# GpSimd takes clamps and remainders of the weights' conversion in the first group, and ELU units are finished in PSUM

## The chip, the cores and the metric

The kernel runs on one core of a Trainium2 chip, as one program. Its engines are TensorE (PE in the profile, with its weight loads as PEld), VectorE (DVE), ScalarE (ACT), GpSimd (POOL), and SyncE (SP), whose queue issues most DMAs. The metric is the device time of one execution in microseconds, the median of three runs.

## The reference

Three stages on 6016 tokens of width 256:

```python
qn = q / (np.linalg.norm(q, axis=1, keepdims=True) + 1e-06)      # over the tokens
kn = k / (np.linalg.norm(k, axis=1, keepdims=True) + 1e-06)
s = kn.transpose(0, 2, 1) @ qn / tau                             # 256 x 256
a = np.exp(s - s.max(-1, keepdims=True)); a /= a.sum(-1, keepdims=True) + 1e-09
x = v @ a                                                        # 6016 x 256
h = x @ w_in                                                     # 256 -> 2048
g = np.where(h > 0, h, np.exp(np.minimum(h, 0)) - 1)             # ELU
x = g @ w_out                                                    # 2048 -> 256
h = x @ w2_in
out = (h / (1 + np.exp(-h))) @ w2_out                            # SiLU
```

The weights arrive as float64 and are read as pairs of 32-bit words.

## The kernel before

First the scores of q and k are summed over all tokens on TensorE, then the softmax is taken and folded into the first layer's input weights, so that the first layer works on v directly. After that the tokens go through layer 1 in six groups of up to 1024 and through layer 2 in six groups again, 12 groups in all. A group has eight steps (`NP`), each for two columns of 128 of the 2048 hidden units. In a step, `first_a` and `first_b` make four units (two halves of the tokens by two columns) of h in the PSUM banks h0 to h3, `unit` turns each into g, and `second` multiplies the g of the step before by the output weights and adds into the four PSUM banks y0 to y3, which hold the group's result over all its steps. Every matrix is held as a high part and a remainder, and a product is three matmuls (high by high, high by low, low by high).

The first group (`plain(n)`, n = 0) differs. Its products are not by a Strassen-like scheme as all others are, so a step has 24 matmuls for h instead of 21, and during it the weights of layer 1 are still being converted. `in_f32` turns a chunk of float64 weights into float32: two copies on ScalarE, a clamp (`ts` with min and max, line 440), a shift (441), the sign (442) and an addition of the low bits (443) on VectorE. `convert` then calls `split`: the high part is a copy on ScalarE, the remainder is a `tt` subtraction on VectorE (line 290). There are 16 chunks, eight of w_in ("w1i") and eight of w_out ("w1o"); the five in `EARLY` are begun ahead of the first step. Chunks of w_in are multiplied by the softmax on TensorE (`m_group`, into h banks), and the result is copied and split again (`m_parts`).

A unit of layer 1 (`unit`, lines 918 to 925) is a chain of five instructions: relu of -h on ScalarE (e from h), exp on ScalarE (e from e), `stt` on VectorE (e from e and h, max(e - 1, h)), a copy on ScalarE to g's high part, and a `tt` on VectorE for g's remainder. h lies in a PSUM bank, e in one of four SBUF buffers.

The first step is special too: its third and fourth unit have no h bank left and are made in y2 and y3 (`first_step`, `y_bank(2), y_bank(3)`). The first `second` then writes y2, y3, y0, y1 in this order. y0 and y1 hold at that time a product of the softmax with the weights (`m_first`), which ScalarE copies out (the rows `h<-y,small`).

The order of the instructions on each engine isn't that of the code. `do` records each one with a cost and with what it reads and writes, and `in_order` then makes a list schedule from a table of costs per engine (`COST`); the engines run what it gives in that fixed order, each waiting at the head of its queue. A PSUM bank is one key: it may be written by the next product when all that read or wrote it for the last one is done.

Of the kernel before, what the change touches and what calls it, by code (L numbers as in the profile page):

```python
# [16 lines left out]
ALU = mybir.AluOpType  # L17
# [4 lines left out]
EARLY = ("w1i", 0), ("w1i", 1), ("w1o", 0), ("w1i", 2), ("w1i", 3)  # L22
# [4 lines left out]
TOP = float(np.array(0x0FEFFFFF, np.uint32).view(np.float32))  # L27
# [16 lines left out]
    "PE": (0.0127, 1 / 2400, 0.22, 0.0),  # L44
    "ACT": (0.14, 1 / 1400, 0.18, 0.12),
    "DVE": (0.067, 1 / 960, 0.15, 0.19),
    "SP": (0.37, 0, 2.3, 0.0),
    "-": (0.0, 0, 0.0, 0.0),
}
# [2 lines left out]
V = namedtuple("V", "ap keys")  # L52
# [102 lines left out]
def channel_attention_elu_silu(  # L155
# [28 lines left out]
    nc = tc.nc  # L184
# [38 lines left out]
    def f32(ap):  # L223
        return ap.bitcast(F32)
# [6 lines left out]
    def do(engine, n, emit, reads, writes, times=1, far=0.0):  # L231
        fixed, each, late, own = DENSE if dense and engine == "ACT" else COST[engine]
        late += far
        ops.append(
            Op(
                engine,
                times * (fixed + each * n),
                late,
                own,
                emit,  # L240
                [k for v in reads if isinstance(v, V) for k in v.keys],
                [k for v in writes for k in v.keys],
                hot,
            )
        )

    def width(ap):
        return int(np.prod(ap.shape[1:]))

    def at(x):  # L250
        return real(x.ap) if isinstance(x, V) else x
# [17 lines left out]
    def tt(out, a, b, op):  # L269
        do("DVE", width(out.ap), lambda: nc.vector.tensor_tensor(at(out), at(a), at(b), op), [a, b], [out])  # L270

    def ts(out, a, s1, s2, *op):
        do("DVE", width(out.ap) / 2, lambda: nc.vector.tensor_scalar(at(out), at(a), at(s1), at(s2), *op), [a, s1, s2], [out])  # L273

    def stt(out, a, s, b, op0, op1):
        emit = lambda: nc.vector.scalar_tensor_tensor(at(out), at(a), at(s), at(b), op0, op1)  # L276
        do("DVE", width(out.ap), emit, [a, s, b], [out])
# [7 lines left out]
        queue, engine = (nc.scalar, "ACT") if by == "ACT" else (nc.sync, "SP")  # L285
        do(engine, 0, lambda: queue.dma_start(at(out), at(src)), [src], [out], n if engine == "SP" else 2 + 3 * short, far)  # L286

    def split(hi, lo, src):
        copy(hi, src)
        tt(lo, src, V(f32(hi.ap), hi.keys), ALU.subtract)  # L290

    def product(out, lhs, rhs, start=True, stop=True, **kw):

# [90 lines left out]
    def wo_at(part, i):  # L384

        also = tuple(("eT", part, d) for d in range(CT)) if i == NP - 1 else ()
        if i in (5, 6):
            also = tuple(("w1i", part, x) for x in range(2))
        return V(wo[part][:, 2 * i : 2 * i + 2], (("wo", part, i), *also))
# [39 lines left out]
    def in_f32(name, i, *order, far=0.0, after=(), wait=()):  # L429


        raw = load(name, i, *order, far=far, after=after)
        low, high = src_of.pop((name, i))
        t = cvs.take()
        a, b = low.ap.shape[1:3]
        w = V(t.ap.rearrange("p (a b) -> p a b", a=a), t.keys)
        wi = V(w.ap.bitcast(I32), t.keys)
        copy(w, V(f32(high.ap), high.keys + wait), scale=2.0**-112)
        copy(low, V(low.ap.bitcast(U32), low.keys + wait), scale=2.0**-29)
        ts(w, w, TOP, -TOP, ALU.min, ALU.max)  # L440
        ts(wi, wi, 3, None, ALU.logical_shift_left)
        stt(wi, V(high.ap, high.keys), SIGN, wi, ALU.bitwise_and, ALU.bitwise_or)
        tt(V(flat(wi.ap), wi.keys), V(flat(wi.ap), wi.keys), V(flat(low.ap), low.keys), ALU.add)
        return w, raw

    def convert(name, i, *order, wait=(), far=LATE[0]):
        w, _ = in_f32(name, i, *order, far=far if order else 0.0, wait=wait)
        if name == "w1i":
            s = slice(i % 2 * HC, (i % 2 + 1) * HC)
            hi, lo = (w1i_at(i // 2, a, slice(None), i % 2) for a in range(2))  # L450
            split(V(hi.ap[:, :, s], hi.keys), V(lo.ap[:, :, s], lo.keys), w)
        else:
            split(wo_at(0, i), wo_at(1, i), w)

    def put_by(name, i, s):

# [33 lines left out]
    with tc.manual_schedule():  # L490
# [87 lines left out]
        for i, (j0, nj) in enumerate(rows):  # L578
            for a, src in enumerate((qv, kv)):
                v = rows_at(a, j0, nj)  # L580
                by = "ACT" if a and i < len(ENDS[0]) else "SP"
                order = ("order",) if by == "SP" else ("order_k",)
# [248 lines left out]
        def plain(n):  # L831

            return n == 0
# [72 lines left out]
        def unit(s, u, h):  # L906
            n, j = steps[s]
            m = cols(n)
            e = cols_of(es.take(), m)
            i = g_free.pop(0)  # L910
            if i < 6:
                g = [V(gs[:, i, a, :m], (("g", i, a),)) for a in range(2)]
            else:
                g = [wa_at(a, i, slice(S1, S4 + 1)) for a in range(2)]
                g = [V(x.ap.flat(), x.keys) for x in g]
            g_at[s, u] = i, g
            if order[n][0] == 1:
                act(e, h, AF.Relu, scale=-1.0)
                act(e, e, AF.Exp, scale=-1.0)
                stt(e, e, -1.0, h, ALU.add, ALU.max)  # L920
                copy(g[0], e)
            else:
                act(g[0], h, AF.Silu)
                act(e, h, AF.Silu)
            tt(g[1], e, V(f32(g[0].ap), g[0].keys), ALU.subtract)
# [328 lines left out]
```

## Time and profile before

| | |
|---|---|
| runs | 1037.5, 1037.96, 1038.38 us; median 1037.96 us |
| span of the profiled execution, first to last instruction | 1035.8 us |
| granted clock of TensorE | 1.00 of full in all 40 slices |
| TensorE busy | 1030.4 us, 99% |
| VectorE, ScalarE, GpSimd busy | 825.1, 749.4, 0.7 us |

The profiled execution's own time isn't listed beside its span; the median of the runs lies 2.2 us above the span, and a difference in the span is carried over to it. Matmuls are pipelined: their listed durations overlap, and it is the distance between starts that tells what one costs. The first group runs from about 53 to 158 us after the span's start.

### The profile page before, as it was taken

The numbers are of one execution on the slowest core, as the hardware profiler recorded it, in microseconds if no ns is written. First come the engines' busy times: TensorE is split into PE (matmuls) and PEld (weight loads), VectorE is DVE, ScalarE is ACT, GpSimd is POOL, SyncE is SP. The second block draws the span as 40 slices with busy tenths as digits, with TensorE's granted clock in tenths as the row PEclk, the third lists the DMA queues.
The fourth block names the chain that finished last, engine by engine and source line by source line (L and its number), as shares of the span: only waits on it lengthen the run. The fifth ranks groups of instructions, "written<-read, shape, count | busy, mean of one in ns | idle before, by whom it ended". The sixth has DMA issues, their size and how long they took to land.

```text
span 1035.8 us, 13366 instructions
## 1 busy us (share of the span) xinstructions
PE 1030.4 (99%) x4734; PEld 872.4 (84%) x4734; DVE 825.1 (80%) x1401; ACT 749.4 (72%) x1410; POOL 0.7 (0%) x6
## 2 busy tenths in 40 slices
PE   9999999999999999999999999999999999999998
PEld 8888888888888888888998888998888888888887
DVE  6999999999989989989998866667566657657553
ACT  6799988989788888888897765565565556555543
POOL 0000000000000000000000000000000000000000
PEclk9999999999999999999999999999999999999999
DMA  9663332033032113013434003012003003001102
GB/s 379 220 173 113 112 71 102 1 72 112 18 75 103 51 46 102 31 42 122 135 97 156 11 1 82 1 41 37 1 4 78 1 1 82 1 1 22 20 1 41
DMA packets 112389, 71.38 MB, mean 69 GB/s; under 512 B 87874, under 2 KB 90562, under 8 KB 111682
## 3 DMA queue, kind: packets, MB, share of 16 engines
q1 hardware_dynamic: 109584, 68.96, 22.6%
q10 hardware_dynamic: 2738, 1.57, 0.5%
q8 instruction: 37, 0.61, 0.3%
q14 instruction: 30, 0.25, 0.1%
HBM read 49.81 MB, written 20.71 MB: 68 GB/s over the span
## 4 chain that ended last, share of the span: by engine, by line
PE 99%; ACT 0%; ACTq 0%; DVE 0%; issue 0%
PE y L297 50%; PE h L297 44%; PE y L324 4%; PE h L311 1%; PE h L324 0%; PE y L311 0%; PE h L329 0%; ACTq L286 0%; ACT big L256 0%; PE y L329 0%; ACT h L256 0%; ACT a L256 0%; DVE a L276 0%; DVE ones L491 0%; ACT e L256 0%
## 5 line engine op out<-in xcount | busy, mean ns | idle before, releaser
L297 PE MATMUL y<-gs,wo 128*128 128x512 f32 (+1 forms) x2196 | 520.5, 385 | 0.0
L297 PEld LDWEIGHTS y<-gs,wo 128*128 128x128 f32 x2196 | 411.8, 188 | 78.1 <-ACT e L256 0.8
L297 PE MATMUL h<-xs,wa 128*128 128x512 f32 (+1 forms) x1980 | 472.6, 385 | 0.0
L297 PEld LDWEIGHTS h<-xs,wa 128*128 128x128 f32 x1980 | 370.9, 188 | 68.5
L270 DVE TENSOR_TENSOR gs<-e,gs 128x512 fp32r<-128x512 f32 (+1 forms) x382 | 253.2, 676 | 90.9 <-ACT e L256 88.6
L270 DVE TENSOR_TENSOR h<-h,h 128x512 f32<-128x512 f32 (+1 forms) x352 | 228.0, 678 | 80.2 <-PE h L297 62.3
L256 ACT ACTIVATE e<-h 128x512 f32<-128x512 f32 (+2 forms) x383 | 225.5, 600 | 46.1 <-DVE h L270 43.5
L256 ACT ACTIVATE h<-h 128x512 f32<-128x512 f32 (+1 forms) x176 | 103.6, 589 | 136.8 <-PE h L297 136.7
L256 ACT ACTIVATE gs<-h 128x512 fp32r<-128x512 f32 (+1 forms) x192 | 116.5, 607 | 70.0 <-DVE h L270 37.7
L276 DVE SCALAR_TENSOR_TENSOR e<-e,h 128x512 f32<-128x512 f32 (+1 forms) x190 | 123.0, 671 | 18.2 <-ACT e L256 17.7
L256 ACT ACTIVATE e<-e 128x512 f32<-128x512 f32 (+1 forms) x192 | 114.0, 623 | 1.3
L256 ACT ACTIVATE gs<-e 128x512 fp32r<-128x512 f32 (+1 forms) x190 | 110.7, 624 | 1.6 <-DVE e L276 1.6
L270 DVE TENSOR_TENSOR xs<-big,xs 128x512 fp32r<-128x512 f32 (+1 forms) x77 | 50.2, 672 | 0.0
L256 ACT ACTIVATE xs<-big 128x512 fp32r<-128x512 f32 (+1 forms) x77 | 45.4, 623 | 1.0 <-DVE big L270 0.7
L270 DVE TENSOR_TENSOR sums<-sums 128x2048 f32<-128x2048 f32 (+3 forms) x17 | 29.4, 1727 | 7.2 <-ACT sums L256 6.2
L273 DVE TENSOR_SCALAR cv<-cv 128x512 f32<-128x512 f32 (+1 forms) x64 | 26.4, 422 | 0.6 <-ACT cv L256 0.3
L297 PEld LDWEIGHTS y<-wo,gs 128*128 128x128 f32 x192 | 24.7, 191 | 1.0
L297 PE MATMUL y<-wo,gs 128*128 128x256 f32 x192 | 25.1, 283 | 0.0
L256 ACT ACTIVATE cv<-st 128x512 f32<-128x512 f32 x32 | 21.4, 674 | 1.5 <-DMA st<-in_moe_w_in_dram 1.5
L324 PE MATMUL y<-ring 128*128 128x256 f32 x92 | 22.3, 395 | 0.0
L276 DVE SCALAR_TENSOR_TENSOR cv<-st,cv 128x512 int32<-128x512 int32 x32 | 21.9, 687 | 0.4
L270 DVE CUSTOM_DVE_ANT_0 cv<-st,cv 128x1024 uint16<-128x1024 uint16 x32 | 21.9, 686 | 0.0
(100 smaller groups left out, 369.6 us busy)
## 6 DMA issues: line engine op xcount, KB each, us to landing
st<-in_moe_w_in_dram SPq DMA_DIRECT2D x16, 512.0 KB, 3.9
st<-in_moe_w_out_dram SPq DMA_DIRECT2D x16, 512.0 KB, 3.8
yd<-e SPq DMA_DIRECT2D x20, 256.0 KB, 2.4
big<-yd SPq DMA_DIRECT2D x5, 1024.0 KB, 4.7
big<-in_v_dram SPq DMA_DIRECT2D x32, 128.0 KB, 3.5
wod<-st SPq DMA_DIRECT2D x8, 512.0 KB, 2.9
wo<-wod SPq DMA_DIRECT2D x8, 512.0 KB, 4.0
out_dram<-big SPq DMA_DIRECT2D x32, 128.0 KB, 2.9
```

The lines of the kernel that those rows point to most:

```text
L256: nc.scalar.activation(at(out), at(src), func, **{k: at(x) for k, x in kw.items()}, **more)
L270: do("DVE", width(out.ap), lambda: nc.vector.tensor_tensor(at(out), at(a), at(b), op), [a, b], [out])
L273: do("DVE", width(out.ap) / 2, lambda: nc.vector.tensor_scalar(at(out), at(a), at(s1), at(s2), *op), [a, s1, s2], [out])
L276: emit = lambda: nc.vector.scalar_tensor_tensor(at(out), at(a), at(s), at(b), op0, op1)
L297: nc.tensor.matmul(at(out), at(lhs[a]), at(rhs[b]), start=start and a + b == 0, stop=stop and a == 1, **kw)
L311: nc.tensor.matmul(at(out), at(both[n][0][a]), at(both[n][1][b]), start=(n, a, b) == (0, 0, 0), stop=(n, a) == (1, 1),)
L324: emit = lambda: nc.tensor.matmul(at(out), at(lhs), at(rhs), start=start, stop=stop, **kw)
```

## The change

Two things. In the first group's conversions, GpSimd now makes the remainders of all eight chunks of w_out and of the six chunks of w_in that aren't the first two (14 subtractions), and the clamps of the eleven chunks that aren't in `EARLY`. `COST` has a row for GpSimd, and the schedule is made anew. And in the first group's units, the `stt` writes its result over h in the PSUM bank instead of into e; the copy and the remainder read it from there.

```diff
--- before.py
+++ after.py
@@ -44,6 +44,7 @@
     "PE": (0.0127, 1 / 2400, 0.22, 0.0),
     "ACT": (0.14, 1 / 1400, 0.18, 0.12),
     "DVE": (0.067, 1 / 960, 0.15, 0.19),
+    "POOL": (0.2, 2.2 / 1000, 0.2, 0.12),
     "SP": (0.37, 0, 2.3, 0.0),
     "-": (0.0, 0, 0.0, 0.0),
 }
@@ -269,7 +270,10 @@
     def tt(out, a, b, op):
         do("DVE", width(out.ap), lambda: nc.vector.tensor_tensor(at(out), at(a), at(b), op), [a, b], [out])
 
-    def ts(out, a, s1, s2, *op):
+    def ts(out, a, s1, s2, *op, pool=False):
+        if pool:
+            do("POOL", width(out.ap) * 0.7, lambda: nc.gpsimd.tensor_scalar(at(out), at(a), at(s1), at(s2), *op), [a], [out])
+            return
         do("DVE", width(out.ap) / 2, lambda: nc.vector.tensor_scalar(at(out), at(a), at(s1), at(s2), *op), [a, s1, s2], [out])
 
     def stt(out, a, s, b, op0, op1):
@@ -285,9 +289,13 @@
         queue, engine = (nc.scalar, "ACT") if by == "ACT" else (nc.sync, "SP")
         do(engine, 0, lambda: queue.dma_start(at(out), at(src)), [src], [out], n if engine == "SP" else 2 + 3 * short, far)
 
-    def split(hi, lo, src):
+    def split(hi, lo, src, pool=False):
         copy(hi, src)
-        tt(lo, src, V(f32(hi.ap), hi.keys), ALU.subtract)
+        if pool:
+            high = V(f32(hi.ap), hi.keys)
+            do("POOL", width(lo.ap), lambda: nc.gpsimd.tensor_tensor(at(lo), at(src), at(high), ALU.subtract), [src, high], [lo])
+        else:
+            tt(lo, src, V(f32(hi.ap), hi.keys), ALU.subtract)
 
     def product(out, lhs, rhs, start=True, stop=True, **kw):
 
@@ -437,7 +445,7 @@
         wi = V(w.ap.bitcast(I32), t.keys)
         copy(w, V(f32(high.ap), high.keys + wait), scale=2.0**-112)
         copy(low, V(low.ap.bitcast(U32), low.keys + wait), scale=2.0**-29)
-        ts(w, w, TOP, -TOP, ALU.min, ALU.max)
+        ts(w, w, TOP, -TOP, ALU.min, ALU.max, pool=order == () and name[:2] == "w1")
         ts(wi, wi, 3, None, ALU.logical_shift_left)
         stt(wi, V(high.ap, high.keys), SIGN, wi, ALU.bitwise_and, ALU.bitwise_or)
         tt(V(flat(wi.ap), wi.keys), V(flat(wi.ap), wi.keys), V(flat(low.ap), low.keys), ALU.add)
@@ -448,9 +456,9 @@
         if name == "w1i":
             s = slice(i % 2 * HC, (i % 2 + 1) * HC)
             hi, lo = (w1i_at(i // 2, a, slice(None), i % 2) for a in range(2))
-            split(V(hi.ap[:, :, s], hi.keys), V(lo.ap[:, :, s], lo.keys), w)
+            split(V(hi.ap[:, :, s], hi.keys), V(lo.ap[:, :, s], lo.keys), w, (name, i) not in EARLY[:2])
         else:
-            split(wo_at(0, i), wo_at(1, i), w)
+            split(wo_at(0, i), wo_at(1, i), w, True)
 
     def put_by(name, i, s):
 
@@ -917,7 +925,11 @@
             if order[n][0] == 1:
                 act(e, h, AF.Relu, scale=-1.0)
                 act(e, e, AF.Exp, scale=-1.0)
-                stt(e, e, -1.0, h, ALU.add, ALU.max)
+                if plain(n):
+                    stt(h, e, -1.0, h, ALU.add, ALU.max)
+                    e = h
+                else:
+                    stt(e, e, -1.0, h, ALU.add, ALU.max)
                 copy(g[0], e)
             else:
                 act(g[0], h, AF.Silu)
```

TensorE's order is the same in both kernels. On the others the rows move. Below, the names are the program's buffers: h0_73 to h3_76 and y0_69 to y3_72 are PSUM banks, e0_111 to e3_114 the SBUF buffers for e, gs the g parts, cv the chunks in float32, st the raw chunks, xs and wo where converted w_in and w_out lie.

ScalarE, first step, right behind the exp of the second unit; before:

```order
L256 ACTIVATE e1_112<-y2_71 128x512
L256 ACTIVATE wo_67<-cv2_110 128x512
L256 ACTIVATE gs_320<-e3_114 128x512
L256 ACTIVATE cv1_109<-st1_106 128x512
L256 ACTIVATE e1_112<-e1_112 128x512
L256 ACTIVATE e2_113<-y3_72 128x512
L256 ACTIVATE xs0_371<-cv0_108 128x2x256
L256 ACTIVATE e2_113<-e2_113 128x512
L256 ACTIVATE st1_106<-st1_106 128x512
L256 ACTIVATE gs_320<-e0_111 128x512
L256 ACTIVATE e3_114<-h0_73 128x512
L256 ACTIVATE h1_116<-y0_69,small_65 128x256
```

And after:

```order
L257 ACTIVATE gs_320<-h2_75 128x512
L257 ACTIVATE e1_112<-y2_71 128x512
L257 ACTIVATE e2_113<-y3_72 128x512
L257 ACTIVATE e1_112<-e1_112 128x512
L257 ACTIVATE gs_320<-h3_76 128x512
L257 ACTIVATE cv1_109<-st1_106 128x512
L257 ACTIVATE wo_67<-cv2_110 128x512
L257 ACTIVATE e2_113<-e2_113 128x512
L257 ACTIVATE xs0_371<-cv0_108 128x2x256
L257 ACTIVATE gs_320<-y2_71 128x512
L257 ACTIVATE st1_106<-st1_106 128x512
L257 ACTIVATE gs_320<-y3_72 128x512
```

The copies to gs of the units in y2_71 and y3_72 stand within these rows now, where before they stand six and seven rows behind them; the copy of y0_69 (`h1_116<-y0_69`) has gone from the last row to five rows behind them.

VectorE at the same place, from the second unit's `stt` on; before:

```order
L276 SCALAR_TENSOR_TENSOR e0_111<-e0_111,h3_76 128x512
L270 TENSOR_TENSOR wo_67<-cv2_110,wo_67 128x512
L270 TENSOR_TENSOR gs_320<-e3_114,gs_320 128x512
L273 TENSOR_SCALAR cv1_109<-cv1_109 128x512
L276 SCALAR_TENSOR_TENSOR e1_112<-e1_112,y2_71 128x512
L273 TENSOR_SCALAR cv1_109<-cv1_109 128x512
L270 TENSOR_TENSOR xs0_371<-cv0_108,xs0_371 128x2x256
L276 SCALAR_TENSOR_TENSOR cv1_109<-st1_106,cv1_109 128x512
L276 SCALAR_TENSOR_TENSOR e2_113<-e2_113,y3_72 128x512
L270 ISA cv1_109<-st1_106,cv1_109 128x1024
L270 TENSOR_TENSOR gs_320<-e0_111,gs_320 128x512
L276 SCALAR_TENSOR_TENSOR e3_114<-e3_114,h0_73 128x512
```

And after:

```order
L280 SCALAR_TENSOR_TENSOR h3_76<-e0_111,h3_76 128x512
L271 TENSOR_TENSOR gs_320<-h2_75,gs_320 128x512
L280 SCALAR_TENSOR_TENSOR y2_71<-e1_112,y2_71 128x512
L271 TENSOR_TENSOR gs_320<-h3_76,gs_320 128x512
L277 TENSOR_SCALAR cv1_109<-cv1_109 128x512 x2
L280 SCALAR_TENSOR_TENSOR y3_72<-e2_113,y3_72 128x512
L280 SCALAR_TENSOR_TENSOR cv1_109<-st1_106,cv1_109 128x512
L271 TENSOR_TENSOR gs_320<-y2_71,gs_320 128x512
L271 ISA cv1_109<-st1_106,cv1_109 128x1024
L271 TENSOR_TENSOR gs_320<-y3_72,gs_320 128x512
L280 SCALAR_TENSOR_TENSOR h0_73<-e3_114,h0_73 128x512
```

Two remainders of weights are gone, the `stt` now write to the banks, and the remainders of g that read y2_71 and y3_72 have come ahead of the next step's units.

GpSimd, whole program but for its first six rows; before:

```order
masks.py:197 MEMSET ident_63 128x128
masks.py:199 ISA
masks.py:199 AFFINE_SELECT ident_63<-ident_63 128x128
L1249 UNCONDITIONAL_BRANCH
L1249 ISA
```

And after, the same rows and the first half of those that are new:

```order
masks.py:199 AFFINE_SELECT ident_63<-ident_63 128x128
L296 TENSOR_TENSOR wo_67<-cv2_110,wo_67 128x512
L296 TENSOR_TENSOR xs0_371<-cv0_108,xs0_371 128x2x256
L296 TENSOR_TENSOR xs0_371<-cv1_109,xs0_371 128x2x256
L275 TENSOR_SCALAR cv2_110<-cv2_110 128x512
L296 TENSOR_TENSOR wo_67<-cv2_110,wo_67 128x512
L275 TENSOR_SCALAR cv0_108<-cv0_108 128x512
L275 TENSOR_SCALAR cv1_109<-cv1_109 128x512
L275 TENSOR_SCALAR cv2_110<-cv2_110 128x512
L296 TENSOR_TENSOR xs0_371<-cv0_108,xs0_371 128x2x256
L296 TENSOR_TENSOR wo_67<-cv2_110,wo_67 128x512
L275 TENSOR_SCALAR cv0_108<-cv0_108 128x512
```

All 25 new instructions stand behind the set-up of the identity matrix, and nothing else is on that queue.

## Rows read from the trace of the kernel before

**Rows 1.** The page, part 1: busy time, share of the span, instructions of each engine.

```profile
PE 1030.4 (99%) x4734; PEld 872.4 (84%) x4734; DVE 825.1 (80%) x1401; ACT 749.4 (72%) x1410; POOL 0.7 (0%) x6
```

**Rows 2.** Windows; columns: stretch, length, busy us (count) by engine, clock, DMA share, GB/s.

```profile
75.00:90.00 15.00, 15.00 (x68) 12.43 (x67) 14.56 (x27) 15.00 (x30) 0.00 (x0) 1.00 0.42 137
90.00:110.00 20.00, 20.00 (x90) 16.58 (x89) 20.00 (x38) 18.87 (x36) 0.00 (x0) 1.00 0.37 110
```

**Rows 3.** Timeline of TensorE, 60 to 75; columns: start us, us, engine, line, operation.

```profile
63.91 3.53 PE L297 MATMUL y<-gs,wo 128*128 128x512 f32 x12
67.28 2.90 PE L311 MATMUL h<-xs,wo 128*128 128x512 f32 x12
70.02 2.88 PE L297 MATMUL y<-gs,wo 128*128 128x512 f32 x12
72.74 1.52 PE L297 MATMUL h<-xs,a 128*128 128x512 f32 x6
```

**Rows 4.** Timeline, 155 to 161: two TensorE rows at the end of the first group.

```profile
156.38 3.42 PE L297 MATMUL y<-gs,wo 128*128 128x512 f32 x12
...
159.64 1.53 PE L297 MATMUL h<-xs,wa 128*128 128x512 f32 x6
```

**Rows 5.** Waits, 55 to 165; columns: who waited for whom: us, times, longest.

```profile
PEld y L297 <- ACT e L256: 0.8, 2, 0.5
...
PEld y L297 <- DVE gs L270: 0.4, 1, 0.4
PEld y L297 <- ACT h L256: 0.4, 1, 0.4
DVE cv L273 <- ACT cv L256: 0.3, 1, 0.3
...
PEld y L297 <- DVE e L276: 0.2, 1, 0.2
```

**Rows 6.** Timeline of ScalarE, 58.3 to 67.

```profile
58.34 0.62 ACT L256 ACTIVATE e<-e 128x512 f32<-128x512 f32 x1
58.86 0.59 ACT L256 ACTIVATE e<-y 128x512 f32<-128x512 f32 x1
59.34 0.63 ACT L256 ACTIVATE wo<-cv 128x512 fp32r<-128x512 f32 x1
...
61.46 0.60 ACT L256 ACTIVATE e<-y 128x512 f32<-128x512 f32 x1
...
62.46 0.65 ACT L256 ACTIVATE e<-e 128x512 f32<-128x512 f32 x1
...
64.53 0.49 ACT L256 ACTIVATE h<-y,small 128x256 f32<-128x256 f32 x1
```

**Rows 7.** Timeline of VectorE, 57 to 70.

```profile
61.61 0.68 DVE L276 SCALAR_TENSOR_TENSOR e<-e,y 128x512 f32<-128x512 f32 x1
...
63.82 0.68 DVE L276 SCALAR_TENSOR_TENSOR e<-e,y 128x512 f32<-128x512 f32 x1
...
65.62 0.68 DVE L276 SCALAR_TENSOR_TENSOR e<-e,h 128x512 f32<-128x512 f32 x1
...
67.61 0.69 DVE L276 SCALAR_TENSOR_TENSOR e<-e,h 128x512 f32<-128x512 f32 x1 [0.70 <-ACT e L256]
```

**Rows 8.** Lines of GpSimd, whole span; columns: busy us, mean ns, idle before.

```profile
masks.py:199 POOL TENSOR_SCALAR_AFFINE_SELECT ident<-ident 128x128 f32<-128x128 f32 x1 | 0.3, 294 | 0.1
...
L1235 POOL MEMSET const-float32-0.0<- 128x1 f32 x1 | 0.1, 99 | 0.2 <-issue 0.2
```

**Rows 9.** Lines of VectorE by form, 55 to 165.

```profile
L270 DVE CUSTOM_DVE_ANT_0 cv<-st,cv 128x1024 uint16<-128x1024 uint16 x14 | 9.6, 688 | 0.0
L276 DVE SCALAR_TENSOR_TENSOR cv<-st,cv 128x512 int32<-128x512 int32 x14 | 9.5, 686 | 0.1
L273 DVE TENSOR_SCALAR cv<-cv 128x512 f32<-128x512 f32 x13 | 5.5, 425 | 0.3 <-ACT cv L256 0.3
L270 DVE TENSOR_TENSOR wo<-cv,wo 128x512 fp32r<-128x512 f32 x8 | 5.5, 688 | 0.1
```

## The prediction

> **What bounds the kernel now.** I read the page's first part, then the windows of the first group (where all the changed rows stand), the waits there, and the timelines of three engines around its first step.
>
> TensorE is listed busy for 99% of the span [rows 1]. That alone says little, since pipelined matmuls overlap; the distance of the starts says more. From 70.02 to 72.74 twelve matmuls of 512 columns start, 2.72 us, 0.227 us each, at a granted clock of 1.00, the 2.4 GHz level [rows 2, 3]. So TensorE is the bound, and only where it waits can time be won. From 55 to 165 us the waits name TensorE in four rows alone [rows 5]; they are found where a block of twelve takes longer than 2.72, at two places. The block at 63.91, the first `second`, takes 3.37 us to the next one at 67.28, 0.65 too much [rows 3]. The block at 156.38, the first of the next group, takes 3.26 us to 159.64, 0.54 too much [rows 4]. In the waits TensorE's weight loads wait for VectorE's `e` and `gs` and for ScalarE's `h` (0.2, 0.4, 0.4) and twice for ScalarE's `e` (0.8), all before writing y [rows 5]. These are waits for a PSUM bank whose last contents somebody still reads. 1.2 us in all, 0.11%, is the most that the change can win in the first group.
>
> VectorE and ScalarE are nearly as full: VectorE shows 20.00 of 20.00 us from 90 to 110, ScalarE 15.00 of 15.00 from 75 to 90 [rows 2]. They run at the edge without holding TensorE up.
>
> **The change part by part.** *Work moved.* 14 remainders at 688 ns and 11 clamps at 425 ns leave VectorE [rows 9]: 9.6 + 4.7 = 14.3 us of its first group. As VectorE isn't what TensorE waits for outside the two places, this is worth nothing by itself; it is room.
>
> *GpSimd's own time.* The trace has no such instruction there. The nearest rows are its 128x128 select with 294 ns and a one-column memset with 99 ns [rows 8]. Scaled to 512 columns that is between 0.10 + 4 x 0.195 = 0.88 and 4 x 0.294 = 1.18 us. I take 1.0, nearer the first, since part of an instruction's time doesn't grow with columns: 25 us in the some 105 us from 60 to 165, a share of 0.24. Its queue holds nothing else, so that it keeps up. The Trainium skill (GPSIMD Engine Reference, § Elementwise — side-by-side cycle accounting) puts a two-input addition on GpSimd at 1.96 times VectorE's time. No run here shows it; by that ratio a remainder would be an estimated 1.35 us, the share 0.28, and the sum below 0.9 us higher.
>
> *Lateness of the clamps.* Behind each clamp VectorE's shift stands at a fixed place in its queue, and all units' `stt` and remainders queue behind the shift. A clamp of 1.0 in place of 0.425 is 0.6 later, and a handover more between engines is about 0.1: 11 x 0.7 = 7.7 us at most. At least it is nothing, or less than nothing, as 4.7 us leave VectorE's queue. The nearest row is VectorE's wait for the copy ahead of the clamp: 0.3 us, once, over 13 chunks [rows 5]. The order leaves enough other work between such steps. I take nothing.
>
> *Two engines side by side.* No row shows VectorE and GpSimd at work together. If they don't disturb each other this costs nothing; a gain beyond the room counted above has no source. At the other end each of VectorE's instructions on the conversion's path, which read two operands from SBUF or run at the faster rate (14 + 14 + 13 = 41 rows [rows 9]), waits out half of a GpSimd instruction when it meets one: 41 x 0.24 x 0.5 = 4.9 us. The remainders of g, which now read one operand from PSUM, I leave out. Both unknown costs together lie between 0 and 12.6. VectorE and ScalarE have no spare time in which a stop would vanish [rows 2], and what stops now stands ahead of the release of a bank; I take 4.9, the lower half of that. The Trainium skill (SBUF — State Buffer, § Who interferes with whom) says that a VectorE instruction with two SBUF inputs, or in a 2-port mode, and one of GpSimd exclude each other for a whole instruction, whoever comes second, and that one with at most one SBUF input is free of it. No run here shows it yet; by it the term stands at its upper end, and the use of PSUM spares the units' remainders.
>
> *Banks held longer.* A bank of a unit was free after the `stt`; now it is free two links later, after ScalarE's copy and VectorE's remainder. At the first `second` this falls on y2 and y3, in which two units were made. Before, TensorE starts on y2 at 63.91 and on y3 at about 64.6, after their `stt` (61.61 to 62.29, 63.82 to 64.50 [rows 7]). After, I follow ScalarE's new order from the exp at 58.34, which both orders have. An instruction starts 0.52 behind one that reads SBUF (58.34 to 58.86) and 0.48 behind one that reads PSUM (58.86 to 59.34) [rows 6]. Gs from h2 58.86, relu y2 59.34, relu y3 59.82, exp 60.30, gs from h3 60.82, cv 61.30, wo 61.82, exp 62.34, xs 62.86, gs from y2 63.38, st 63.86, gs from y3 64.38. With 0.6 for each copy and 0.06 for the handover VectorE's remainders can start at 64.04 and 65.04; between them stands the low-bit addition, which needs the st copy's end. So they run at about 64.25 and 65.45, and y2 and y3 are free at 64.9 and 66.1 instead of 62.29 and 64.50. The copies of y0 and y1, which TensorE needs next, come later too: relu h0 64.86, exp 65.52 (it waits for the relu), xs 66.04, relu h1 66.56, copy of y0 67.04, exp 67.40, gs from h0 67.92, copy of y1 68.40 to 68.89 (0.49, [rows 6]). TensorE may write y1 at 68.95. Before, it did so three matmuls ahead of 67.28, near 66.5 (67.28 - 0.68 = 66.6, a bit less by its wait). **+2.4 us**, and all that TensorE does stands behind it.
>
> Elsewhere the h banks had between 0.3 and 1 us to spare at this time: `stt` ends of 66.30 and 68.30 [rows 7] against writes at 67.28 and 67.28 + 6 x 0.227 = 68.64 [rows 3]. Two more links, 0.48 + 0.60 + handovers, are some 1.3 us; TensorE's own delay of 2.4 covers this in all later steps. The waits at 157 to 159 (0.54) I take as gone, since VectorE has room by then: -0.5. Behind the first group the instructions are the same, if partly in other places, and TensorE's 99% [rows 1] leave little there. The copies to gs read PSUM, 0.48 instead of 0.52: 32 x 0.04 = 1.3 us of ScalarE, hidden under TensorE. SP's queue changes places among a few loads and stores of intermediate weights; they have several us of lead, and I count nothing.
>
> Sum: 2.4 - 0.5 + 4.9 = +6.8 us on a span of 1035.8. Carried over to the median of 1037.96: **1044.8 us**.
>
> **The rivals.** *The bank wait alone.* GpSimd works beside VectorE without harm, and the 14.3 us of room hide its lateness: 2.4 - 0.5 = +1.9, 1039.9 us. For it speaks that only 0.3 us of waiting for a conversion is seen now [rows 5]; against it, that three engines at their limits have nowhere to put a stop.
>
> *VectorE's room comes first.* The chain of the first step is held up in the trace by VectorE's queue: the exp of y3 ends at 63.11, its `stt` starts at 63.82 [rows 6, 7]. If the 14.3 us make this chain, and ScalarE's that waits on it, faster than I followed it by more than 1.9 us, no bank is late and the two waits go: -1.2 to 0, 1036.8 to 1038. It decides from the point at which the remainder of y3 ends before about 64.6. Against it: ScalarE's order alone, without any wait, puts the copy ahead of it at 64.38.
>
> *Both unknown costs at their ends.* Each late clamp is a stop of VectorE and reaches TensorE: 1.9 + 12.6 = +14.5, 1052.5 us. Against it speaks the 0.3 of [rows 5].
>
> **How the numbers follow.** The measurement tells 0.2%, 2.1 us, from no change. The forecast, slower by 3 to 12 us, has 0.53; the bank wait alone, +1 to +3, has 0.28, of which six tenths are within 2.1 us; VectorE's room first has 0.12, of which 0.02 are faster by over 2.1 us (which needs a source that I don't see); both ends, over +12, has 0.07. Slower: 0.53 + 0.07 + 0.11 = 0.71; the same: 0.17 + 0.10 = 0.27; faster 0.02. The range leaves out the fast rival and the worst of the last: 1038.9 to 1051.0. The forecast's own is 1041 to 1050.
>
> **What would show it.** In the changed profile the first `second` should start near 65 instead of 63.91 and its last block of three near 69, with TensorE waiting for VectorE's gs and ScalarE's h. If these starts are as before, the chain is wrong. GpSimd should show 25 instructions of 0.9 to 1.2 us; well over that means that they wait. Instructions of VectorE such as the shift or the sign should show some lengthened cases or idle time ended by GpSimd, and TensorE waits for h banks between 70 and 160. If VectorE's means stay at 688 and 425 ns and no such wait is there, the term of 4.9 is wrong and the time is near 1040. The blocks from 160 us on should keep their distance.

## The result, and the profile after

The changed kernel takes 1045.13 us (median of 5 runs, 1044.83 to 1045.36), the kernel before 1037.79 beside it (5 runs): ratio 1.0071, 95% interval 1.0059 to 1.0083. It is slower by 7.3 us; the profiled spans are 1043.2 and 1035.8 us, +7.4.

The page's busy line of the changed kernel, which answers to [rows 1]:

```profile
PE 1031.6 (99%) x4734; PEld 871.2 (84%) x4734; DVE 824.0 (79%) x1376; ACT 749.3 (72%) x1410; POOL 28.7 (3%) x31
```

VectorE has 25 instructions fewer, 14.3 us by [rows 9], yet its busy time fell by only 1.1 us. So what is left takes longer, and takes back most of the room. What became longer is found by instruction form, here of VectorE from 55 to 165 us (columns as in [rows 9]); in this order the forms had 688 (then from e), 688, 686 and 424 ns before:

```profile
L271 DVE TENSOR_TENSOR gs<-h,gs 128x512 fp32r<-128x512 f32 x28 | 19.0, 683 | 2.9 <-ACT gs L257 2.6
L271 DVE CUSTOM_DVE_ANT_0 cv<-st,cv 128x1024 uint16<-128x1024 uint16 x14 | 11.4, 822 | 0.0
L280 DVE SCALAR_TENSOR_TENSOR cv<-st,cv 128x512 int32<-128x512 int32 x14 | 10.3, 749 | 0.1
L277 DVE TENSOR_SCALAR cv<-cv 128x512 int32<-128x512 int32 x13 | 8.4, 655 | 1.1 <-POOL cv L275 1.1
```

The remainders of g, which now read one operand from PSUM, kept their time. The conversion's three kinds became longer, by 14 x 0.134 + 14 x 0.063 + 13 x 0.231 = 5.8 us. In the same view four more forms, with both operands in SBUF, lengthened by 3.1 us: `h<-cv,h` from 286 to 410 ns, `xs<-big,xs` from 687 to 757, `big<-big,big` from 684 to 1229 and `big<-big` from 686 to 932 (8, 7, 2 and 2 instructions). Together that is 8.9 us. GpSimd's own rows, 40 to 175 us, sum to 28.1 us:

```profile
L296 POOL TENSOR_TENSOR wo<-cv,wo 128x512 fp32r<-128x512 f32 x8 | 12.0, 1501 | 79.3 <-ACT wo L257 79.3
L296 POOL TENSOR_TENSOR xs<-cv,xs 128x512 fp32r<-128x512 f32 x6 | 8.2, 1359 | 11.0 <-ACT xs L257 4.9 <-DVE cv L277 4.8 <-issue 1.4
L275 POOL TENSOR_SCALAR cv<-cv 128x512 f32<-128x512 f32 x11 | 7.9, 726 | 15.1 <-ACT cv L257 15.1
```

The timeline of TensorE around the first `second`, which answers to [rows 3]; the bracket is idle time and who ended it:

```profile
66.62 0.96 PE L305 MATMUL y<-gs,wo 128*128 128x512 f32 x3 [2.41 <-DVE gs L271]
67.82 1.87 PE L305 MATMUL y<-gs,wo 128*128 128x512 f32 x6 [0.24 <-DVE gs L271]
70.10 0.96 PE L305 MATMUL y<-gs,wo 128*128 128x512 f32 x3 [0.41 <-ACT h L257]
70.90 2.89 PE L319 MATMUL h<-xs,wo 128*128 128x512 f32 x12
```

y2 starts at 66.62 instead of 63.91, after a wait for the remainder of a unit's g, and the block of h behind it at 70.90 instead of 67.28: +3.6 us. I use that block, the L311 row of [rows 3], as the yardstick for every kernel below; the lag is how much later the same matmul starts than in the trace of the kernel before. A part of each lag is there at 15 us, ahead of all changed rows: 0.2 us in the changed kernel, 0.6 in the PSUM half below (where TensorE waits 0.55 and 0.22 us for the DMA of k) and with the remainders only, 0.3 or less in the others. It says nothing of the change and is to be taken off. The rest of the loss comes in the later steps. TensorE's waits between 95 and 130 us, where the trace before has none:

```profile
97.14 1.66 PE L319 MATMUL h<-xs,wo 128*128 128x512 f32 x6 [0.23 <-DVE gs L271]
103.16 0.96 PE L305 MATMUL h<-xs,a 128*128 128x512 f32 x3 [0.62 <-DVE gs L271]
122.95 3.02 PE L319 MATMUL h<-xs,wo 128*128 128x512 f32 x12 [1.14 <-DVE gs L271]
129.62 0.72 PE L305 MATMUL h<-xs,a 128*128 128x512 f32 x2 [0.25 <-DVE gs L271]
```

These are h banks that VectorE's remainder of g still reads. The lag is 3.6 us from the yardstick on, grows at these four waits to 4.1, 5.4, 6.8 and 7.4, hardly between them, and is still 7.4 at 156 (time before). A wait costs more than the idle time in its bracket, which begins only at the modelled end of the matmul before. The first block of the next group then starts regularly; the two rows that answer to [rows 4]:

```profile
163.76 2.88 PE L305 MATMUL y<-gs,wo 128*128 128x512 f32 x12
166.49 1.75 PE L305 MATMUL h<-xs,wa 128*128 128x512 f32 x7
```

They are 2.73 us apart, not 3.26: the waits there went, and the lag falls from 7.4 to 6.9. It is 7.4 again at the end: between 170 and 400 us three weight loads of TensorE wait, 0.9 us in all (0.4 for ScalarE's `e`, 0.3 and 0.2 for VectorE's `e` and `h`), where the trace before has no wait.

What GpSimd and VectorE do to each other is seen on the timeline of the stretch that holds TensorE up:

```profile
62.31 1.98 DVE L277 TENSOR_SCALAR cv<-cv 128x512 f32<-128x512 f32 x2
62.71 1.30 POOL L296 TENSOR_TENSOR wo<-cv,wo 128x512 fp32r<-128x512 f32 x1 [61.41 <-ACT wo L257]
63.54 0.61 ACT L257 ACTIVATE gs<-y 128x512 fp32r<-128x512 f32 x1
63.96 1.46 POOL L296 TENSOR_TENSOR xs<-cv,xs 128x512 fp32r<-128x512 f32 x1
64.21 0.68 DVE L280 SCALAR_TENSOR_TENSOR y<-e,y 128x512 f32<-128x512 f32 x1
64.81 1.16 DVE L280 SCALAR_TENSOR_TENSOR cv<-st,cv 128x512 int32<-128x512 int32 x1
64.93 0.60 ACT L257 ACTIVATE gs<-y 128x512 fp32r<-128x512 f32 x1 [0.22 <-DVE y L280]
65.89 0.68 DVE L271 TENSOR_TENSOR gs<-y,gs 128x512 fp32r<-128x512 f32 x1
67.09 0.68 DVE L271 TENSOR_TENSOR gs<-y,gs 128x512 fp32r<-128x512 f32 x1
```

Two VectorE instructions of 0.42 us take 1.98 together beside GpSimd's first remainder, and end 0.3 us behind it (64.29 against 64.01). The next GpSimd remainder runs to 65.42, and the sign, 0.69 us otherwise, takes 1.16 and ends at 65.97. Between them the `stt` of y3, with one operand in PSUM, keeps its 0.68. Both stops stand ahead of the remainder of y2 at 65.89 and so of TensorE's start at 66.62.

### The profile page after: what moved, and what is told of

Same layout as the page of the kernel before. It is cut to its first block, busy times and chain, and to the rows that moved or that the text cites. A ratio compares the mean times of both kernels' runs of the same rounds, so it can differ in the third digit from the quotient of the medians.

```text
span 1043.2 us, 13369 instructions
## 1 busy us (share of the span) xinstructions
PE 1031.6 (99%) x4734; PEld 871.2 (84%) x4734; DVE 824.0 (79%) x1376; ACT 749.3 (72%) x1410; POOL 28.7 (3%) x31
## 4 chain that ended last, share of the span: by engine, by line
PE 92%; DVE 4%; ACT 2%; issue 1%; DMA 1%; POOL 0%; ACTq 0%; DVEq 0%
PE y L305 47%; PE h L305 41%; PE y L332 4%; DVE h L280 1%; DVE cv L271 1%; DMA ring<-in_k_dram 1%; ACT e L257 1%; DVE gs L271 1%; DVE cv L280 1%; ACT gs L257 0%; PE h L319 0%; DVE big L271 0%; DVE big L284 0%; DVE cv L277 0%; ACT cv L257 0%
## 5 line engine op out<-in xcount | busy, mean ns | idle before, releaser
L305 PEld LDWEIGHTS h<-xs,wa 128*128 128x128 f32 x1980 | 370.7, 188 | 68.9 <-DVE e L280 0.3
L271 DVE TENSOR_TENSOR gs<-e,gs 128x512 fp32r<-128x512 f32 (+1 forms) x352 | 232.8, 674 | 92.5 <-ACT e L257 88.7
L257 ACT ACTIVATE gs<-h 128x512 fp32r<-128x512 f32 (+1 forms) x220 | 133.5, 608 | 74.7 <-DVE h L271 37.6
L280 DVE SCALAR_TENSOR_TENSOR e<-e,h 128x512 f32<-128x512 f32 (+1 forms) x160 | 102.5, 667 | 17.7 <-ACT e L257 17.1
L257 ACT ACTIVATE gs<-e 128x512 fp32r<-128x512 f32 (+1 forms) x160 | 92.7, 623 | 0.0
L277 DVE TENSOR_SCALAR cv<-cv 128x512 int32<-128x512 int32 (+1 forms) x53 | 24.9, 477 | 1.3 <-POOL cv L275 1.1
```

The costliest lines, as they stand in the source:

```text
L257: nc.scalar.activation(at(out), at(src), func, **{k: at(x) for k, x in kw.items()}, **more)
L305: nc.tensor.matmul(at(out), at(lhs[a]), at(rhs[b]), start=start and a + b == 0, stop=stop and a == 1, **kw)
```

## The experiments

Two theories. The banks (BANK): a unit's PSUM bank is held two links longer, and TensorE waits for it. The stops (STOP): VectorE instructions that meet a GpSimd instruction wait until it ends. Rivals to the second: clamps that come late from GpSimd's queue, or the new order of all engines (the schedule is made anew for each edit, so that most kernels below differ in order too; TensorE's order is the same in all). The lag is given at the yardstick and, as the difference of the profiled spans, at the end.

**The PSUM half alone.** Clamps and remainders stay on VectorE:

```diff
-        ts(w, w, TOP, -TOP, ALU.min, ALU.max, pool=order == () and name[:2] == "w1")
+        ts(w, w, TOP, -TOP, ALU.min, ALU.max, pool=False)
...
-            split(wo_at(0, i), wo_at(1, i), w, True)
+            split(wo_at(0, i), wo_at(1, i), w)
```

(and the same for w_in).

> The PSUM half of the change alone: the stt writes over h in the first group, GpSimd does nothing. Theory BANK (TensorE loses because a bank comes free two links later): the wait ahead of the first second's y blocks stays, its last block of three starts 2 to 3 us later than before (66.48), 1040 to 1041 us. Theory STOP (VectorE stops while GpSimd works): without GpSimd nothing is stopped, VectorE's means stay at 688 and 425 ns, at most +0.5, near 1038 us.

Measured: 1040.37 us, ratio 1.0024 (1.0014 to 1.0034). TensorE's timeline:

```profile
65.48 0.96 PE L305 MATMUL y<-gs,wo 128*128 128x512 f32 x3 [0.84 <-DVE gs L271]
66.68 1.84 PE L305 MATMUL y<-gs,wo 128*128 128x512 f32 x6 [0.24 <-DVE gs L271]
69.48 0.96 PE L305 MATMUL y<-gs,wo 128*128 128x512 f32 x3 [0.96 <-ACT h L257]
70.28 3.01 PE L319 MATMUL h<-xs,wo 128*128 128x512 f32 x12
```

The lag is 3.0 at the yardstick and 3.3 at the end, of which 0.6 were there before; VectorE's means stay at 681 to 688 and 419 ns. Behind this block of h TensorE's weight loads wait only twice until 157 us, 0.5 us in all: the banks, with the order made for them, cost nearly all of it in the first `second`.

**The GpSimd half alone.** The unit's `stt` writes to e as before:

```diff
-                if plain(n):
+                if False:
```

> The GpSimd half alone: e stays in SBUF, 25 instructions on GpSimd. BANK: no bank is held longer, 0 to 1 us less than before, 1037 to 1038. STOP: VectorE's conversion steps lengthen as in the changed kernel (shift 655, sign 749, low bits 822 ns), and the remainders of g, which now read two operands from SBUF, lengthen too, above 720 ns; +3 to +6, 1041 to 1044 us.

Measured: 1045.09 us, ratio 1.0068 (1.0053 to 1.0083); the lag is 1.0 at the yardstick, 3.3 at 118, 6.5 at the end (the profiled execution took 1044.11 us, 1.0 below the median). VectorE's rows by form:

```profile
L271 DVE TENSOR_TENSOR gs<-e,gs 128x512 fp32r<-128x512 f32 x34 | 24.5, 730 | 0.9 <-ACT gs L257 0.8
L280 DVE SCALAR_TENSOR_TENSOR e<-e,h 128x512 f32<-128x512 f32 x34 | 22.9, 680 | 6.1 <-ACT e L257 6.0
L280 DVE SCALAR_TENSOR_TENSOR cv<-st,cv 128x512 int32<-128x512 int32 x14 | 12.8, 911 | 0.2
```

The sign takes 911 ns instead of 686; `stt` with h in PSUM keeps 680. The low bits (686) and the shift (446) hardly lengthen, against the expectation: which instructions meet GpSimd differs from order to order. And the loss is above the range expected: this half alone costs what both cost together. So the halves don't add (2.6 and 7.3 make 7.3). Two reasons fit, and no run tells them apart. Here the remainders of g read two SBUF operands and are stopped too, 730 against 688 ns; with e in PSUM they are spared. And what TensorE loses at the first `second` can shorten its later waits: in the next run the yardstick's lag falls by 1.8 us, that at the end by 0.3.

**The y units' e in SBUF**, in the changed kernel and in the PSUM half:

```diff
-                if plain(n):
+                if plain(n) and h.keys[0][0] != "y":
```

> The changed kernel, but the two units of the first step that lie in y2 and y3 keep their e in SBUF. BANK: the wait at the first second falls from 3.6 us to the 0.7 of before, 1042 us. STOP: the stt of these units is itself late behind lengthened shifts, so that at least half of the wait stays, 1043.5 to 1045 us.

> The PSUM half alone, but the two units in y2 and y3 keep their e in SBUF. BANK: nearly all of the 3.1 us of the PSUM half's span came at the first second, from these two units; without them the block starts near 63.9 and 66.5 as before, 1037.3 to 1038.3 us. If the h banks matter as well: 1039 or more.

Measured: the changed kernel with it 1044.69 us (1.0067, 1.0052 to 1.0082), the PSUM half 1039.87 (1.0019, 1.0009 to 1.0028). The yardstick's lag falls from 3.6 to 1.8 and from 3.0 to 1.7, yet at the end it is 7.1 and 2.7. In the PSUM half TensorE now waits for ScalarE's copies of y0 and y1:

```profile
66.28 0.97 PE L305 MATMUL y<-gs,wo 128*128 128x512 f32 x3 [0.43 <-ACT h L257]
68.17 0.98 PE L305 MATMUL y<-gs,wo 128*128 128x512 f32 x3 [0.92 <-ACT h L257]
```

The changed kernel does what STOP expected. The PSUM half doesn't return to the time before; it is in the range of its second branch, 1039 or more. Behind the two copies TensorE's weight loads for h wait for VectorE as well, seven times from 71 to 157 us, 2.4 us in all. Taking away the wait for y2 and y3 gives back little, because the chain behind it, ScalarE's order and the h banks, is late too.

**Work on GpSimd that nobody needs**, in the kernel before: each of the 14 conversions is followed by a GpSimd subtraction that reads two 128x512 operands from SBUF and writes into a buffer that nobody reads. TensorE's and SyncE's orders are those of before, VectorE's and ScalarE's differ in a few rows.

```diff
+        if dummy:
+            high = V(f32(hi.ap), hi.keys)
+            junk = V(idle.rearrange("p (a b) -> p a b", a=2), ("idle",))
+            do("POOL", width(lo.ap), lambda: nc.gpsimd.tensor_tensor(at(junk), at(high), at(high), ALU.subtract), [high], [junk])
```

> The kernel before, and beside each of the 14 remainders GpSimd makes a subtraction of the high part from itself into a buffer that nobody reads; nothing waits for it. BANK: 1038 us, as before. STOP: VectorE's instructions with two SBUF operands lengthen (means of remainders of g above 720 ns), VectorE has no room for it, and TensorE waits: +2 to +6, 1040 to 1044 us.

Measured: 1043.06 us, ratio 1.0051 (1.0034 to 1.0068), though no instruction waits for GpSimd's result. VectorE's rows by form, GpSimd's last:

```profile
L272 DVE TENSOR_TENSOR gs<-e,gs 128x512 fp32r<-128x512 f32 x34 | 25.0, 750 | 0.2 <-ACT gs L258 0.2
L278 DVE SCALAR_TENSOR_TENSOR e<-e,h 128x512 f32<-128x512 f32 x34 | 22.6, 677 | 1.2 <-ACT e L258 1.2
...
L272 DVE TENSOR_TENSOR xs<-cv,xs 128x512 fp32r<-128x512 f32 x6 | 7.1, 1180 | 0.0
L272 DVE TENSOR_TENSOR wo<-cv,wo 128x512 fp32r<-128x512 f32 x8 | 6.6, 820 | 0.1
...
L295 POOL TENSOR_TENSOR idle<-xs 128x512 bf16<-128x512 f32 x6 | 8.6, 1440 | 28.0 <-ACT xs L258 28.0
```

The remainders that start beside GpSimd's subtraction of the same chunk take 1180 ns instead of 687; `stt` with h in PSUM keeps 677. One meeting on the timeline, GpSimd and VectorE:

```profile
62.70 1.21 POOL L295 TENSOR_TENSOR idle<-xs 128x512 bf16<-128x512 f32 x1 [2.11 <-ACT xs L258]
```

```profile
62.93 1.52 DVE L272 TENSOR_TENSOR xs<-cv,xs 128x512 fp32r<-128x512 f32 x1
```

GpSimd ends at 63.91, VectorE 0.54 later, so that most of its 0.69 us of work came behind GpSimd's. The `stt` of y3 stands behind it, and TensorE waits for that:

```profile
65.71 2.63 PE L303 MATMUL y<-gs,wo 128*128 128x512 f32 x9 [0.97 <-DVE e L278]
```

The result is as STOP expected.

**Writes only.** The same, but each subtraction is cut to one column and followed by three memsets of 512 columns. Every other engine has the order of the run with subtractions, row by row:

```diff
+                nc.gpsimd.tensor_tensor(idle[:, 0:1], real(one_col), real(one_col), ALU.subtract)
+                for _ in range(3):
+                    nc.gpsimd.memset(idle, 0.0)
```

> The kernel before with GpSimd work beside each remainder as in the run with subtractions, but it only writes: one subtraction of one column, then three memsets of 512 columns into a buffer that nobody reads. If VectorE stops because GpSimd reads SBUF: remainders of g stay near 688 ns and the time is within 0.6 us of 1037.8; the shift, at its faster rate, may lengthen. If any GpSimd work stops VectorE, about as long per us of GpSimd's work as before: +2 or more.

Measured: 1037.99 us, ratio 1.0001 (0.9992 to 1.001), with 33 us of GpSimd work:

```profile
L272 DVE TENSOR_TENSOR gs<-e,gs 128x512 fp32r<-128x512 f32 x34 | 22.6, 681 | 0.2 <-ACT gs L258 0.2
...
L299 POOL MEMSET idle<- 128x512 bf16 x42 | 22.3, 531 | 2.4
```

The two runs differ in GpSimd's instructions alone. So it is GpSimd's reading of SBUF that stops VectorE's instructions with two SBUF operands, and with it STOP is shown; the new order that both runs share costs nothing. The shift, which reads one operand, lengthened a little, 446 against 424 ns.

**Which of GpSimd's instructions.** The changed kernel with only the clamps on GpSimd, and with only the remainders:

```diff
-            split(wo_at(0, i), wo_at(1, i), w, True)
+            split(wo_at(0, i), wo_at(1, i), w)
```

(the first, and the same for w_in) and

```diff
-        ts(w, w, TOP, -TOP, ALU.min, ALU.max, pool=order == () and name[:2] == "w1")
+        ts(w, w, TOP, -TOP, ALU.min, ALU.max, pool=False)
```

> The changed kernel with only the 11 clamps on GpSimd (0.73 us each, 8 us) and the 14 remainders on VectorE. The remainders read two operands and take 1.4 us each, 20 us: if the stops go with the time that GpSimd reads, the clamps give 0.29 of the GpSimd half's 4.9, +2.5 + 1.4, 1041.7 us; if the clamps are what hurts because shift, sign and the units queue behind them, 1043.5 or more.

> The changed kernel with its clamps back on VectorE, so that GpSimd makes only the 14 remainders; the units' e stays in PSUM. If the remainders' reads of two SBUF operands are what costs (the clamps alone cost nothing beyond the PSUM half), the time is that of the changed kernel, 1043.5 to 1046, and VectorE's two-SBUF-input rows are lengthened as there. If the clamps' lateness and the remainders' work only cost together, it is 1040 to 1042.

Measured: clamps only 1040.41 us (1.0024, 1.0015 to 1.0034), lag 2.6 at the yardstick and 2.7 at the end, as the PSUM half; remainders only 1044.54 (1.0066, 1.0051 to 1.0081), lag 4.7 and 6.9 (the 4.7 holds a stretch of lower clock, told in the last section). The clamps alone cost nothing, less than either figure expected; the remainders, as expected, cost nearly what the change costs, some 4 us beyond the banks (1044.54 - 1040.37 = 4.2).

**The order.** The changed kernel's order, with the 25 instructions issued on VectorE at the place where GpSimd's were recorded:

```diff
-            do("POOL", width(out.ap) * 0.7, lambda: nc.gpsimd.tensor_scalar(at(out), at(a), at(s1), at(s2), *op), [a], [out])
+            do("POOL", width(out.ap) * 0.7, lambda: nc.vector.tensor_scalar(at(out), at(a), at(s1), at(s2), *op), [a], [out])
```

(and the same for the subtraction).

> The changed kernel's order on every engine, but the 25 instructions run on VectorE, at the place in its queue that the schedule gave them on GpSimd. VectorE gets the 14.3 us of work back; nothing runs on GpSimd. If the cost of the GpSimd half is the stops (STOP), the time is that of the PSUM half alone, +2 to +3.5, 1040 to 1041.3 us. If it is the new order itself, or VectorE's lack of room, it stays at 1044.5 or more.

Measured: 1046.24 us, ratio 1.008 (1.0065 to 1.0095); lag 3.6 and 8.7 (the 3.6 with a stretch of lower clock too), with VectorE's means at 680 and 416 ns. The expectation failed: an order that counts on 14.3 us less on VectorE costs as much when VectorE does the work as when it is stopped. The PSUM half does the same work on the same engines in another order and takes 1040.37 us: the changed order costs 5.9 us more when it lacks the room that it counts on. The run can't tell the order from the room, so two more keep the order and the room and take away the remainders' stops. Each GpSimd remainder becomes one column and three memsets of zeros, or one memset:

```diff
-            do("POOL", width(lo.ap), lambda: nc.gpsimd.tensor_tensor(at(lo), at(src), at(high), ALU.subtract), [src, high], [lo])
+            def emit():
+                nc.gpsimd.tensor_tensor(col(lo), col(src), col(high), ALU.subtract)
+                for _ in range(3):
+                    nc.gpsimd.memset(real(f32(lo.ap)), 0.0)
+
+            do("POOL", width(lo.ap), emit, [src, high], [lo])
```

> The changed kernel with its order on every engine, but each of GpSimd's 14 subtractions is cut to one column, followed by three memsets that fill the remainder with zeros (so the remainders of these chunks are left out): GpSimd still works about 1.7 us for each, the waits on it stay, but it reads almost nothing. If GpSimd's reads stop VectorE (the stops), VectorE's means go back to some 684 to 690 and 420 to 450 ns and the time to that of the PSUM half, 1040 to 1041. If it is the new order, or GpSimd's lateness, that costs, the time stays at 1044 to 1046 with the means short.

> As the run with three memsets, but one memset for each of the 14 remainders (which are again left out): GpSimd works about 0.85 us for each, so that a clamp behind one is hardly late; the order is the changed kernel's. The run with three memsets stood at 1042.7. If the part of its loss beyond the banks (some 2 us) comes from clamps that wait behind GpSimd's long remainders, the time falls to 1040 to 1041.3 and VectorE's wait for GpSimd's clamps (2.1 us there) goes. If it is the order itself that costs, the time stays at 1042.2 to 1043.

Measured: 1042.72 us (1.0048, 1.0031 to 1.0065) and 1041.85 (1.0038, 1.0026 to 1.0051); lag 2.7 and 2.8 at the yardstick, 5.1 and 4.0 at the end. From 749, 822 and 655 ns in the changed kernel, VectorE's sign, low bits and shift fall to 681, 709 and 544 with three memsets and to 703, 738 and 480 with one; GpSimd's clamps still read SBUF. Neither expectation of the first held: it lies between them. Its timeline shows what is left, GpSimd and VectorE:

```profile
75.81 1.69 POOL L303 MEMSET wo<- 128x512 f32 x3
77.48 1.19 POOL L275 TENSOR_SCALAR cv<-cv 128x512 f32<-128x512 f32 x2
```

```profile
78.13 0.82 DVE L277 TENSOR_SCALAR cv<-cv 128x512 int32<-128x512 int32 x1 [1.73 <-POOL cv L275]
```

Two clamps stand in GpSimd's queue behind a remainder, and VectorE waits 1.73 us for the first of them. Its wait for clamps is 2.1 us in all with three memsets, 0.6 with one, 1.1 in the changed kernel. The second run with 1041.85 lies a little above its range for "late clamps" and below the one for "order": some 0.9 us is likely lateness (the two intervals overlap, the single runs don't), and up to 1.5 (1041.85 against 1040.37) stays with the order or what is left of the clamps' work on GpSimd. Behind the yardstick TensorE has one wait in that run, 0.62 us at 101.46 for VectorE's gs.

**A version that might gain.** Only the clamps on GpSimd, e in SBUF as before:

```diff
-                if plain(n):
-                    stt(h, e, -1.0, h, ALU.add, ALU.max)
-                    e = h
-                else:
-                    stt(e, e, -1.0, h, ALU.add, ALU.max)
+                stt(e, e, -1.0, h, ALU.add, ALU.max)
```

(on top of the clamps-only kernel).

> The kernel before with only the 11 clamps on GpSimd: the remainders stay on VectorE, the units' e in SBUF. Since the clamps cost nothing beyond the PSUM half, and the banks are free as early as before, this takes 4.7 us off VectorE without a stop. If VectorE's room is worth anything, the 0.65 us wait at the first second shrinks: 1037.0 to 1037.8. If the new order or the handovers cost what the room gives, it is 1037.8 to 1039.

Measured: 1038.4 us, ratio 1.0005 (0.9996 to 1.0014), lag 0.1 throughout the first group and 0.9 at the end: no difference that can be told, and no gain. The 0.9 comes behind 165 us, where weight loads wait as in the changed kernel. 4.7 us of work taken off VectorE buy nothing; no kernel here is faster than the one before.

## Why the prediction was right, and where its terms were off

The time, 1045.1 against 1044.8 forecast, came from the two mechanisms of the sum. The first term is right in detail; that the second comes out so near is partly luck.

- **Banks, +2.4.** Right in place and size. Less the 0.6 that were there before, the PSUM half lags 2.4 at the yardstick, and its y2 and y1 start at 64.9 and 68.9, where the chain has 64.9 and 68.95; the changed order with GpSimd nearly idle lags 2.5. The chain was right about what is late (gs, then ScalarE's copy of y1). In the changed kernel y2 starts at 66.62 and the last block of three at 70.10: the two stops on VectorE's queue ahead of the remainder of y2 come on top, 0.9 us (3.4 against 2.5).
- **"These are waits for a PSUM bank."** Three of the four rows are. The 0.4 for `gs` stands, by the count of weight loads, within y0's three matmuls, whose first had begun, so that it was a wait for the remainder itself. The bound of 1.2 us doesn't hang on it.
- **"TensorE's own delay of 2.4 covers this in all later steps."** Nearly true for the banks alone, where the lag grows by 0.3 us behind the yardstick, and with the clamps taken off VectorE besides, by 0.1. Beside the stops it fails: in the changed kernel the waits at 97, 103, 123 and 130 us are h banks, and 3.8 us come after the yardstick.
- **Waits at 157 to 159, -0.5.** Right: 3.26 became 2.73. Behind the group the prediction counted nothing; there the weight loads' waits between 170 and 400 us lost 0.5 again.
- **Stops, +4.9.** The mechanism is shown by the unneeded subtractions. What GpSimd's part adds to the PSUM half is 4.8 (1045.13 against 1040.37), but not for stops alone: the changed kernel against the same order with memsets is 2.4 us (one that writes longer) or 3.3 (one that writes less), and lateness and order are the rest. Nor did every stop reach TensorE, as "no spare time in which a stop would vanish" has it: VectorE's instructions became 8.9 us longer, 5.8 on the conversion's rows, more than the 4.9 forecast, and at most 4.8 reached TensorE. Two errors met: too small a sum of stops, and too large a share of it passed on. The unit remainders, left out of the 41 rows, were rightly left out: 683 ns.
- **Lateness of clamps, 0 of at most 7.7.** Nearly right: VectorE waits for a clamp once, 1.1 us, and three memsets against one cost 0.9 in time. It and the 1.5 us that stay with the order fill up what the stops lacked.
- **GpSimd's own time, 25 us.** 28.1, with another split: remainders 1.36 to 1.50 instead of 1.0 us, clamps 0.73. The means of the remainders hold waits for VectorE; the one at 62.71, for which VectorE waits, takes 1.30. The Trainium skill (GPSIMD Engine Reference, § Elementwise — side-by-side cycle accounting) puts a two-input addition of 2048 columns at 1.96 times VectorE's time, which gives an estimated 1.35 us here; the trace agrees.

The Trainium skill (SBUF — State Buffer, § Who interferes with whom) says that a VectorE instruction with two SBUF inputs contends with a GpSimd instruction that reads SBUF, not with one that only writes it, and that with one input outside its faster modes it is free of it. The runs agree on each: 750 and 1180 ns beside reads, 681 beside memsets, 677 for `stt` with h in PSUM. The prediction left out that the GpSimd instruction must read, and took the rule for the upper end of the term; VectorE's stops went beyond that end, the loss of TensorE stayed below it.

Of the rivals, the bank wait alone (1039.9) is what the PSUM half shows, 1040.37, and falls for the whole change; VectorE's room first falls, as the remainder of y3 ends at 67.77 and not before 64.6, and y2 is late in every kernel that keeps e in its bank; both ends (1052.5) falls with the clamps' small lateness.

What stays open: how the 1.5 us between the PSUM half and the order with one memset divide between the order and GpSimd's remaining work, and why the two halves together cost no more than the GpSimd half.

## What to carry to other kernels

Before work is moved to GpSimd, count VectorE's instructions beside it that take two operands from SBUF: each that meets a GpSimd instruction that reads waits until it is done, or holds it up; 14 reading subtractions that nobody needed cost 5.2 us by that alone. Putting one operand into PSUM spares an instruction the stop, but a result that stays in a PSUM bank holds the bank until its last reader, and where TensorE writes there next it pays for that. Room on an engine that the bound engine doesn't wait for is worth nothing, here 4.7 us without any gain; but an order made for that room costs dearly where the room is lacking, here 5.9 us.

## What the runs showed of the hardware

- TensorE's granted clock fell for a few microseconds after its wait at the first `second` in two profiled runs: to 0.50, the 1.2 GHz level, from 67 to 70 us in the run with all work on VectorE (the wait before it 1.94 us), and from 69 to 71 in the run with the remainders only (2.42 us). The changed kernel's profile, with a wait of 2.41 us, shows 1.00 there. Windows of the first two (columns as in [rows 2]):

```profile
67.00:70.00 3.00, 2.94 (x7) 2.15 (x7) 2.73 (x5) 3.00 (x7) 0.00 (x0) 0.50 0.66 182
```

```profile
69.00:71.00 2.00, 2.00 (x6) 1.47 (x5) 1.29 (x2) 2.00 (x6) 0.57 (x1) 0.50 0.94 281
```

  In the second, nine matmuls from 68.20 to 71.95 take 3.75 us instead of 2.04. The time of the whole hardly shows it: runs of these two kernels with a mean clock of 0.998 take 1046.17 to 1046.63 and 1044.36 to 1044.88 us, those with 1.000 take 1046.2 and 1044.52; of the changed kernel's five, the three with 0.998 take 1045.13 to 1045.36, the two others 1044.83 and 1045.03. That fits with later waits that become shorter when TensorE is late here; only the mean clock of the unprofiled runs is known.
- 33 us of GpSimd memsets and one-column subtractions beside a full VectorE cost nothing (1.0001); 20 us of subtractions that read cost 5.2 us.
- Stops go both ways: in the run with the unneeded subtractions one GpSimd subtraction that starts at 89.06 takes 2.47 us, where five others take 1.04. Beside it VectorE runs three instructions with two SBUF operands in a row, from 88.74, 89.34 and 89.95, at their usual 0.68 us each; two of them start after GpSimd's:

```profile
89.06 2.47 POOL L295 TENSOR_TENSOR idle<-xs 128x512 bf16<-128x512 f32 x1 [11.93 <-ACT xs L258]
...
92.19 1.04 POOL L295 TENSOR_TENSOR idle<-xs 128x512 bf16<-128x512 f32 x1 [0.66 <-ACT xs L258]
```

- The shift, with one SBUF input at the faster rate, is stopped as well: 0.82 us at 78.13 beside a clamp on GpSimd, 0.42 alone.
- VectorE's `stt` and remainder take the same time with the result or one operand in PSUM: 685 and 683 ns against 684 and 688 in SBUF.
